# The second unit over tiles of 512 tokens, which may span two batches, in place of halves of 288 tokens of one batch

## The chip, the core and the metric

One core of one Trainium2 chip. The metric is the device time of one execution in microseconds; the value shown for a kernel is the median of its runs. The profile is one further execution of the same program, recorded by the hardware.

## What is computed

Causal attention with a cumulative bias (4 batches, 8 heads, 576 tokens, 64 wide), then a gated unit with a token-mixing matrix (the first unit), then a squared-ReLU unit with a sigmoid gate (the second unit). The second unit, which the change is about, cut to what matters:

```python
B, S, D = x.shape                      # 4, 576, 512: 2304 tokens in all
x_prev = concatenate([zeros((B, 1, D)), x[:, :-1, :]], axis=1)   # the token before, 0 at each batch's start
xk = mu_k * x + (1.0 - mu_k) * x_prev
xr = mu_r * x + (1.0 - mu_r) * x_prev
k = maximum(xk @ w_k, 0.0)             # 512 -> 1024
v = k * k @ w_v                        # 1024 -> 512
r = 1.0 / (1.0 + exp(-(xr @ w_r)))     # 512 -> 512
return r * v
```

## The kernel before

Features lie on the 128 partitions, tokens along the free dimension. Products are made in three terms: each float32 operand is split into a part that the matmul format holds and the remainder ("hi" and "lo"; `split_lo` makes the remainder by a subtraction), and for each 128-row block of the contraction the helper `gemm3` issues hi·hi, lo·hi and hi·lo into one PSUM bank.

Attention (`attn_pair`) and the first unit (`moe1`, one call for each batch b) run interleaved. `moe1(b)` ends with four output blocks: for each m, two halves of 288 tokens are accumulated (`o`), VectorE adds the residual into an SBUF tile `y` of 577 columns, whose column 0 was set to zero by GpSimd, and one DMA writes `y` to the DRAM tensor `ydram[m, :, b]` (L464). The zero column stands for the token before the first.

The second unit starts when attention has given its SBUF back. `late(i)` loads a 512 KB piece of the weights `w_k`, `w_r` or `w_v` (tile `lraw`, two buffers) and converts it from 64-bit words to hi and lo, on ScalarE and VectorE (`convert`, with the tiles `ly` and `lz`). Then, batch by batch:

- `prep(b)`: for each feature block k one DMA brings `yt` (577 columns) from `ydram`; for xk and for xr ScalarE multiplies the shifted columns 0 to 575 (`lt`, L563), VectorE adds the columns 1 to 576 times mu (L564), ScalarE copies the hi part (L565), and the lo part is a subtraction, on VectorE for batch 0 and on GpSimd for the others (L566).
- `k`: for 8 blocks m and 2 halves of 288 tokens, 12 matmuls into a bank, ReLU by ScalarE to `lk`, square by VectorE, hi copy `kh` by ScalarE, lo part `kl` by VectorE.
- `gate(m)` (`r`, sigmoid to `sg`) and `vo`: for 4 blocks m and 2 halves, 12 and 24 matmuls; VectorE multiplies and a DMA writes 576 columns to the output.

That is 192 + 96 + 192 = 480 matmuls of 288 columns for a batch, 1920 in all. The eight PSUM banks are handed out in turn (`bank`); `y`, `lk` and `o` share three SBUF buffers (tag `tmp`), `lt` has four and `yt` two.

All DMAs are issued by SyncE (SP), one queue in program order: an entry whose wait isn't over holds up those behind it. The order on each engine is made by a list scheduler when the program is built, from dependences and its own estimate of time.

Of the kernel before, what the change touches and what calls it, by code (L numbers as in the profile page):

```python
# [37 lines left out]
def fused_kernel(ctx, tc, kqT, vL, s, w_in, g_ln, w_sgT, b_sg, w_out, mu_k, mu_r, w_k, w_v, w_r, out):  # L38
# [5 lines left out]
    ydram = dram.tile([KD, P, B, S + 1], F32, tag="ydram", name="ydram")  # L44
# [314 lines left out]
    def moe1(b):  # L359
# [87 lines left out]
        for m in range(KD):  # L447
# [16 lines left out]
            nc.sync.dma_start(out=ydram[m, :, b], in_=y)  # L464
# [83 lines left out]
    def late(i):  # L548
        src, (hi, lo) = loads[i]
        raw = lw.tile([P, 512, 2], U32, tag="lraw", name=f"lraw{i}", bufs=2)  # L550
        nc.sync.dma_start(out=raw.rearrange("p n c -> p (n c)"), in_=src.bitcast(U32))
        y = lw.tile([P, S], F32, tag="ltmp", name=f"ly{i}", bufs=4)
        t = lw.tile([P, S], F32, tag="ltmp", name=f"lz{i}", bufs=4)
        convert(hi, lo, raw, y[:, :512], t[:, :512].bitcast(U32), nc.vector, low=mhalf[:, 0:1])

    def prep(b):
        xx = [[ep.tile([P, KD, S], F32R, tag=t, name=f"x{t}_{b}") for t in r] for r in (("vn0", "vn1"), ("xs0", "xs1"))]
        for k in range(KD):
            yt = lw.tile([P, S + 1], F32, tag="yt", name=f"yt{b}_{k}", bufs=2)
# [8 lines left out]

    for b in range(B):
        if b == 0:  # L570
            for i in range(8):
# [8 lines left out]
        for m in range(KF):  # L580
            f = slice(m * P, (m + 1) * P)
            if b == 0:
# [1 line left out]
            t = ep.tile([P, S + 1], F32, tag="tmp", name=f"lk{b}_{m}", bufs=3)[:, :S]
# [13 lines left out]
        def gate(m):
            f = slice(m * P, (m + 1) * P)
            sg[m] = ew.tile([P, S], F32, tag="wc", name=f"sg{b}_{m}", bufs=3)  # L600
            for hf in range(2):
                acc = bank(f"r{b}_{m}_{hf}")
                c = slice(hf * HF, (hf + 1) * HF)
                mms = []
                for k in range(KD):
                    mms += [(wr[0][:, k, f], xr[0][:, k, c]), (wr[0][:, k, f], xr[1][:, k, c]), (wr[1][:, k, f], xr[0][:, k, c])]
                gemm3(acc[:, :HF], mms)
                nc.scalar.activation(sg[m][:, c], acc[:, :HF], AF.Sigmoid, scale=1.0 / WS)

        gate(0)  # L610
        for m in range(KD):
# [3 lines left out]
            o = ep.tile([P, S + 1], F32, tag="tmp", name=f"o{b}_{m}", bufs=3)[:, :S]  # L615
            for hf in range(2):
                acc = bank(f"vo{b}_{m}_{hf}")
                c = slice(hf * HF, (hf + 1) * HF)
                mms = []
                for k in range(KF):  # L620
                    mms += [(wvv[0][k][:, f], kk[0][k][:, c]), (wvv[0][k][:, f], kk[1][k][:, c]), (wvv[1][k][:, f], kk[0][k][:, c])]
                gemm3(acc[:, :HF], mms)
                nc.vector.scalar_tensor_tensor(out=o[:, c], in0=acc[:, :HF], scalar=1.0 / WS, in1=sg[m][:, c], op0=ALU.mult, op1=ALU.mult)  # L623
# [48 lines left out]
```

## Time and profile before

| | before |
|---|---|
| median of 3 runs | 714.98 us (714.29 to 715.26) |
| span of the profiled execution | 714.3 us |
| TensorE matmul busy | 674.2 us, 94% |
| VectorE / ScalarE / GpSimd busy | 429.2 / 394.7 / 248.9 us |

In the profile PE is TensorE's matmuls, PEld its weight loads, DVE VectorE, ACT ScalarE, POOL GpSimd, SP SyncE. Times within the execution count from the span's start. Matmuls overlap, so the cost of one within a run of them is the distance between starts, not its listed duration. The granted clock is in shares of 2.4 GHz (1.00 is 2.4 GHz, 0.50 is 1.2 GHz).

### The profile page before, as it was taken

How to read it: one execution, taken by the hardware profiler on the slowest of the kernel's cores; microseconds unless marked ns; L12 is line 12 of the kernel's file. 1: busy time of each engine (PE TensorE's matmuls, PEld its weight loads, DVE VectorE, ACT ScalarE, POOL GpSimd, SP SyncE). 2: the span in 40 equal slices, each digit the busy share in tenths (PEclk: the TensorE clock that was granted, in tenths of full speed). 3: DMA queues.
4: the chain of work that ended last, by engine and by line, in shares of the span. 5: the costliest groups of instructions: out<-in, count | busy, mean ns of one | idle time of the engine just before them, and what ended most of it. 6: DMA issues, size and time to landing. Idle time of an engine off the chain costs nothing.

```text
span 714.3 us, 12830 instructions
## 1 busy us (share of the span) xinstructions
PE 674.2 (94%) x4720; PEld 603.2 (84%) x4720; DVE 429.2 (60%) x952; ACT 394.7 (55%) x911; POOL 248.9 (35%) x243
## 2 busy tenths in 40 slices
PE   2869999999998999999999999999999999999998
PEld 1546767878976888977988999899999999999997
DVE  6876589994668455479733589898434144413411
ACT  4777787874557555367734587598435134512400
POOL 7455555367246268245463130002402030330000
PEclk9989999999999899999999999999999999999999
DMA  7663551552733332742401873652300120000001
GB/s 209 190 220 91 163 151 49 171 159 65 211 94 96 112 83 69 196 127 64 128 15 44 287 237 114 202 171 83 90 30 16 52 68 1 17 33 19 2 21 46
DMA packets 33038, 74.96 MB, mean 105 GB/s; under 512 B 4368, under 2 KB 8464, under 8 KB 32976
## 3 DMA queue, kind: packets, MB, share of 16 engines
q1 hardware_dynamic: 32976, 74.15, 34.4%
q8 instruction: 37, 0.61, 0.4%
q14 instruction: 25, 0.20, 0.1%
HBM read 50.84 MB, written 13.79 MB: 90 GB/s over the span
## 4 chain that ended last, share of the span: by engine, by line
PE 78%; DVE 10%; DMA 5%; issue 2%; POOL 2%; ACT 2%; SPq 0%; DVEq 0%; POOLq 0%; ACTq 0%
PE k L355 14%; PE vo L355 14%; PE pv L326 8%; PE r L355 7%; PE sg L355 6%; PE v L355 5%; PE tp L296 5%; PE o L355 4%; PE u L355 4%; PE sc L247 4%; PE sc L248 3%; DMA kq<-in_kqT_dram 3%; DMA lraw<-in_w_k_dram 2%; DVE st L272 1%; DVE QB L224 1%
## 5 line engine op out<-in xcount | busy, mean ns | idle before, releaser
L355 PE MATMUL k<-xvn,wk 128*128 128x288 f32 x768 | 102.9, 295 | 0.4 <-DVE y L461 0.4
L355 PEld LDWEIGHTS k<-xvn,wk 128*128 128x128 f32 x768 | 102.2, 188 | 0.7 <-DVE y L461 0.7
L247 PE MATMUL sc<-ka,qa 128*128 128x512 f32 (+3 forms) x180 | 64.3, 368 | 26.5 <-DVE mx L272 12.6
L280 ACT ACTIVATE st<-st,mx 128x128 f32<-128x128 f32 (+4 forms) x124 | 72.0, 583 | 21.8 <-DVE mx L272 20.7
L272 DVE CUSTOM_DVE_ANT_0 st<-sc,mask 128x512 f32<-128x512 f32 (+3 forms) x124 | 61.0, 501 | 15.8 <-PE sc L248 12.3
L326 PE MATMUL pv<-pt,vf 128*64 128x320 f32 (+4 forms) x448 | 68.3, 380 | 0.7 <-DVE u L484 0.6
L247 PEld LDWEIGHTS sc<-ka,qa 128*128 128x128 f32 x180 | 33.5, 187 | 41.4 <-DVE mx L272 17.6
L355 PE MATMUL sg<-wsg,vn 128*128 128x288 f32 x448 | 65.2, 298 | 1.2 <-DVE u L484 1.2
L355 PEld LDWEIGHTS sg<-wsg,vn 128*128 128x128 f32 x448 | 60.6, 188 | 2.3 <-DVE u L484 1.5
L623 DVE SCALAR_TENSOR_TENSOR o<-vo,sg 128x288 f32<-128x288 f32 x32 | 14.5, 456 | 79.8 <-PE vo L355 79.6
L66 POOL TENSOR_TENSOR KB<-kq,ka 64x576 fp32r<-64x576 f32 x29 | 44.0, 1516 | 48.9 <-ACT ka L225 44.4
L326 PEld LDWEIGHTS pv<-pt,vf 128*64 128x64 f32 x448 | 36.7, 142 | 27.1 <-issue 7.7
L66 POOL TENSOR_TENSOR xvn<-lt,xvn 128x576 fp32r<-128x576 f32 x12 | 19.8, 1658 | 111.6 <-ACT xvn L565 111.6
L248 PE MATMUL sc<-KB,QB 128*128 128x512 f32 (+3 forms) x180 | 58.5, 337 | 0.0
L355 PE MATMUL vo<-kh,wva 128*128 128x288 f32 x256 | 56.2, 295 | 0.0
L355 PE MATMUL vo<-kh,wvb 128*128 128x288 f32 x256 | 56.1, 295 | 0.0
L66 POOL TENSOR_TENSOR qa<-kq,QB 64x576 fp32r<-64x576 f32 x29 | 43.1, 1486 | 33.7 <-DVE QB L224 21.7
L592 ACT ACTIVATE lk<-k 128x288 f32<-128x288 f32 x64 | 26.2, 409 | 49.0 <-PE k L355 46.9
L355 PE MATMUL r<-xxs,wr 128*128 128x288 f32 x384 | 52.9, 295 | 0.0
L355 PEld LDWEIGHTS r<-xxs,wr 128*128 128x128 f32 x384 | 51.6, 188 | 0.0
L296 PE MATMUL tp<-ident,st 128*128 128x128 f32 x300 | 47.4, 277 | 1.8 <-ACT rb L339 1.4
L355 PE MATMUL v<-wv,xs 128*128 128x512 f32 x192 | 48.7, 397 | 0.0
(176 smaller groups left out, 1566.6 us busy)
## 6 DMA issues: line engine op xcount, KB each, us to landing
wc<-wscr SPq DMA_DIRECT2D x24, 512.0 KB
kq<-in_kqT_dram SPq DMA_DIRECT2D x32, 288.0 KB
vf<-in_vL_dram SPq DMA_DIRECT2D x16, 320.0 KB
ydram<-y SPq DMA_DIRECT2D x16, 288.5 KB
yt<-ydram SPq DMA_DIRECT2D x16, 288.5 KB
out_dram<-o SPq DMA_DIRECT2D x16, 288.0 KB
qa<-QB SPq DMA_DIRECT2D x30, 144.0 KB
ka<-ka SPq DMA_DIRECT2D x30, 144.0 KB
```

The costliest lines, as they stand in the source:

```text
L66: eng.tensor_tensor(out=lo, in0=x, in1=f32(hi), op=ALU.subtract)
L224: (nc.scalar.copy if hd < 2 else nc.vector.tensor_copy)(qb[64:128], kq[64:128])
L247: nc.tensor.matmul(sc[:m, :c1 - c0], qa[:, q], ka[:, c0:c1], start=True, stop=False)
L248: nc.tensor.matmul(sc[:m, :c1 - c0], qb[:, q], kb[:, c0:c1], start=False, stop=True)
L272: nc.vector.tensor_tensor_reduce(out=st[:, c0:c1], in0=sc[:, :n], in1=mk, op0=ALU.add, op1=ALU.min, scale=-SCALE, scalar=mx[:, 0:1] if ci ...
L280: e = nc.scalar.activation(st[:, :w], st[:, :w], AF.Exp, bias=mx[:, last:last + 1], scale=-1.0, accum_out=sm[:, 4 * hh + i % 4:4 * hh + i ...
L296: nc.tensor.transpose(tp[:, c:c + P], st[:, j * P:(j + 1) * P], ident)
L326: nc.tensor.matmul(acc[64 * a:64 * a + 64, o:n], vf[:, a, kk], pt, start=(kk == 0), stop=(kk == nk - 1))
L355: nc.tensor.matmul(acc, a, w_, start=(i == 0), stop=(i == n - 1))
L592: nc.scalar.activation(t[:, c], acc[:, :HF], AF.Relu, scale=1.0 / WS)
L623: nc.vector.scalar_tensor_tensor(out=o[:, c], in0=acc[:, :HF], scalar=1.0 / WS, in1=sg[m][:, c], op0=ALU.mult, op1=ALU.mult)
```

## The change

The second unit no longer goes by batches. The 2304 tokens are taken as one row and cut into four tiles of 512 and one of 256 (`CH`, `TOK`); a tile may hold the end of one batch and the start of the next. Every accumulation covers a whole tile: 96 + 48 + 96 = 240 matmuls a tile, 960 of 512 columns and 240 of 256, and one evacuation in place of two. So that the shifted tokens of a tile that spans two batches can be read without a special case, `ydram` holds y twice: copy 0 the tokens, copy 1 the tokens shifted by one, with the zero at each batch's start. Each `y` tile is therefore written by two DMAs of 288 KB, and `yt` is read as two rows of 512 columns (512 KB; 256 KB for the last tile). The lo parts of `prep` are all made by VectorE.

```diff
-    ydram = dram.tile([KD, P, B, S + 1], F32, tag="ydram", name="ydram")
+    ydram = dram.tile([2, KD, P, B * S], F32, tag="ydram", name="ydram")
...
-            nc.sync.dma_start(out=ydram[m, :, b], in_=y)
+            for i in range(2):
+                nc.sync.dma_start(out=ydram[i, m, :, b * S:(b + 1) * S], in_=y[:, 1 - i:1 - i + S])
...
-            yt = lw.tile([P, S + 1], F32, tag="yt", name=f"yt{b}_{k}", bufs=2)
-            nc.sync.dma_start(out=yt, in_=ydram[k, :, b])
+            yt = lw.tile([P, 2, CH], F32, tag="yt", name=f"yt{c}_{k}", bufs=2)
+            nc.sync.dma_start(out=yt[:, :, :n], in_=ydram[:, k, :, t0:t0 + n].rearrange("i p n -> p i n"))
...
-                nc.scalar.mul(t, yt[:, 0:S], mu[:, r, 1, k:k + 1])
-                nc.vector.scalar_tensor_tensor(out=t, in0=yt[:, 1:S + 1], scalar=mu[:, r, 0, k:k + 1], in1=t, op0=ALU.mult, op1=ALU.add)
-                nc.scalar.copy(xx[r][0][:, k], t)
-                split_lo(nc.gpsimd if b else nc.vector, xx[r][1][:, k], t, xx[r][0][:, k])
+                nc.scalar.mul(t, yt[:, 1, :n], mu[:, r, 1, k:k + 1])
+                nc.vector.scalar_tensor_tensor(out=t, in0=yt[:, 0, :n], scalar=mu[:, r, 0, k:k + 1], in1=t, op0=ALU.mult, op1=ALU.add)
+                nc.scalar.copy(xx[r][0][:, k, :n], t)
+                split_lo(nc.vector, xx[r][1][:, k, :n], t, xx[r][0][:, k, :n])
...
-    for b in range(B):
+    for c in range((TOK + CH - 1) // CH):
+        n = min(CH, TOK - c * CH)
+        t0 = c * CH
...
-            for hf in range(2):
-                acc = bank(f"k{b}_{m}_{hf}")
-                c = slice(hf * HF, (hf + 1) * HF)
-                mms = []
-                for k in range(KD):
-                    mms += [(wk[0][:, k, f], xk[0][:, k, c]), (wk[0][:, k, f], xk[1][:, k, c]), (wk[1][:, k, f], xk[0][:, k, c])]
-                gemm3(acc[:, :HF], mms)
-                nc.scalar.activation(t[:, c], acc[:, :HF], AF.Relu, scale=1.0 / WS)
+            acc = bank(f"k{c}_{m}")
+            mms = []
+            for k in range(KD):
+                xh, xl = (x[:, k, :n] for x in xk)
+                mms += [(wk[0][:, k, f], xh), (wk[0][:, k, f], xl), (wk[1][:, k, f], xh)]
+            gemm3(acc[:, :n], mms)
+            nc.scalar.activation(t, acc[:, :n], AF.Relu, scale=1.0 / WS)
...
-            nc.sync.dma_start(out=out[m, :, b], in_=o)
+            nc.sync.dma_start(out=out[m].rearrange("p b s -> p (b s)")[:, t0:t0 + n], in_=o)
```

`gate` and `vo` change in the same way as `k`.

SP's queue at the place where the first weight pieces are loaded (`y_0` to `y_3` are batch 2's outputs, `wc_` the weights of batch 3's first unit, `lraw` pieces of `w_k`, `yt_` the tokens of the first tile). Before:

```order
L464 DMA ydram<-y_0_4651 128x577
L551 DMA lraw_5335<-in_w_k_dram 128x1024
L551 DMA lraw_5345<-in_w_k_dram 128x1024
L560 DMA yt_0_5419<-ydram 128x577
L560 DMA yt_1_5431<-ydram 128x577
L492 DMA wc_0_4796<-wscr 128x1024
L464 DMA ydram<-y_1_4702 128x577
L551 DMA lraw_5355<-in_w_k_dram 128x1024
```

After:

```order
L465 DMA ydram<-y_0_4659 128x576 x2
L552 DMA lraw_5351<-in_w_k_dram 128x1024
L552 DMA lraw_5361<-in_w_k_dram 128x1024
L566 DMA yt_0_5435<-ydram 128x2x512
L566 DMA yt_1_5447<-ydram 128x2x512
L493 DMA wc_0_4808<-wscr 128x1024
L465 DMA ydram<-y_1_4711 128x576 x2
L552 DMA lraw_5371<-in_w_k_dram 128x1024
```

The sequence is the same; each `y` entry stands twice and each `yt` carries 512 KB where it carried 288.

TensorE's row in the first batch or tile, where `vo` first needs the converted `w_v` (`wva` its first four blocks, `wvb` its last four). Before, at the end of `vo_0`:

```order
L355 MATMUL vo_0_1_5941<-kl_6_5518,wvb_5333 128x288
L355 MATMUL vo_0_1_5941<-kh_6_5513,wvb_5334 128x288
L355 MATMUL vo_0_0_5915<-kh_7_5514,wvb_5334 128x288
L355 MATMUL vo_0_1_5941<-kh_7_5514,wvb_5333 128x288
L355 MATMUL vo_0_1_5941<-kl_7_5519,wvb_5333 128x288
L355 MATMUL vo_0_1_5941<-kh_7_5514,wvb_5334 128x288
L355 MATMUL r_2_0_5969<-xxs_0_5417,wr_5329 128x288
```

After, where `vo_0` first reads `wvb`:

```order
L355 MATMUL r_2_5819<-xxs_0_5434,wr_5345 128x512
L355 MATMUL r_2_5819<-xxs_0_5433,wr_5346 128x512
L355 MATMUL vo_1_5834<-kh_0_5523,wva_5347 128x512
L355 MATMUL vo_0_5791<-kh_4_5527,wvb_5349 128x512
L355 MATMUL vo_0_5791<-kl_4_5532,wvb_5349 128x512
L355 MATMUL vo_1_5834<-kl_5531,wva_5347 128x512
L355 MATMUL vo_1_5834<-kh_0_5523,wva_5348 128x512
L355 MATMUL vo_0_5791<-kh_4_5527,wvb_5350 128x512
```

Before, `r_2` came after the whole of `vo_0`; now its 12 matmuls and half of `vo_1` stand ahead of `vo_0`'s use of `wvb`.

## Rows read from the trace of the kernel before

**Rows 1.** The page: span, busy time (share) xinstructions of two engines.

```profile
span 714.3 us, 12830 instructions
PE 674.2 (94%) x4720; PEld 603.2 (84%) x4720; DVE 429.2 (60%) x952; ACT 394.7 (55%) x911; POOL 248.9 (35%) x243
```

**Rows 2.** Chain that ended last, one batch and the end: start us, us, what.

```profile
583.46 25.49 PE k L355 x192
...
647.12 25.49 PE k L355 x192
...
698.08 12.73 PE vo L355 x96
```

**Rows 3.** PE's waits from 395 to 715 us: us in total, times, longest.

```profile
PE o L355 <- DVE gl L66: 1.8, 1, 1.8
PE k L355 <- DVE y L461: 0.4, 1, 0.4
```

**Rows 4.** Timeline of PE and PEld: start us, us, op, shape, xcount [idle before <-releaser].

```profile
404.49 6.09 PE L355 MATMUL v<-wv,xs 128*128 128x512 f32 x26
410.41 2.02 PE L355 MATMUL v<-wv,xq 128*128 128x512 f32 x8
412.27 12.89 PE L355 MATMUL u<-xs,wc 128*128 128x288 f32 x96
425.00 15.26 PE L355 MATMUL sg<-wsg,vn 128*128 128x288 f32 x112
...
427.78 1.36 PEld L355 LDWEIGHTS sg<-wsg,vn 128*128 128x128 f32 x10 [0.21 <-DVE vn L66]
```

**Rows 5.** Timeline of PE at 219 us, two matmuls of 256 columns.

```profile
219.00 0.28 PE L247 MATMUL sc<-ka,qa 128*128 128x256 f32 x1
219.12 0.28 PE L248 MATMUL sc<-KB,QB 128*128 128x256 f32 x1
```

**Rows 6.** Windows: PE, PEld, DVE, ACT, POOL busy (x), PEclk, DMA share, GB/s.

```profile
402.00:404.00 2.00, 2.00 (x14) 1.83 (x14) 1.77 (x5) 0.88 (x2) 0.00 (x0) 1.00 1.03 403
404.00:406.00 2.00, 2.00 (x12) 1.74 (x12) 1.84 (x5) 1.89 (x2) 0.00 (x0) 1.00 1.02 415
...
446.00:448.00 2.00, 0.45 (x3) 0.45 (x4) 2.00 (x4) 1.53 (x3) 0.10 (x1) 1.00 0.00 0
452.00:454.00 2.00, 1.56 (x12) 1.42 (x11) 2.00 (x7) 1.29 (x3) 0.00 (x0) 1.00 0.98 317
...
570.00:580.00 10.00, 10.00 (x78) 10.00 (x77) 5.54 (x6) 5.71 (x9) 6.71 (x4) 1.00 0.17 52
```

**Rows 7.** Timeline of ACT; in brackets idle us before it and its releaser.

```profile
406.95 0.67 ACT L73 ACTIVATE ly<-lraw 128x512 f32<-128x512 f32 x1 [0.33 <-DMA lraw<-in_w_k_dram]
...
461.40 0.67 ACT L73 ACTIVATE ly<-lraw 128x512 f32<-128x512 f32 x1 [1.81 <-DMA lraw<-in_w_r_dram]
```

**Rows 8.** Timeline of DVE, load stage and first batch.

```profile
433.98 0.75 DVE L66 TENSOR_TENSOR xxs<-lt,xxs 128x576 fp32r<-128x576 f32 x1
...
462.75 0.69 DVE L79 SCALAR_TENSOR_TENSOR lz<-lraw,lz 128x512 uint32<-128x512 uint32 x1 [1.92 <-ACT lz L78]
...
492.53 0.69 DVE L66 TENSOR_TENSOR wvb<-ly,wvb 128x512 fp32r<-128x512 f32 x1
```

**Rows 9.** The end: last piece of the chain that ended last.

```profile
710.89 0.46 DVE o L623
```

**Rows 10.** Timeline of SP from 705 us: start us, us from first to last.

```profile
705.03 6.68 SPq L624 DMA_DIRECT2D out_dram<-o  x2
```

**Rows 11.** Windows of 1 us around a fall of the granted clock, columns as above.

```profile
228.00:229.00 1.00, 0.00 (x0) 0.00 (x0) 1.00 (x5) 0.27 (x1) 1.00 (x1) 1.00 0.44 78
229.00:230.00 1.00, 0.74 (x2) 0.30 (x2) 1.00 (x4) 0.73 (x3) 0.46 (x1) 0.84 0.72 247
231.00:232.00 1.00, 1.00 (x3) 0.22 (x1) 1.00 (x5) 0.09 (x1) 0.22 (x1) 0.50 0.00 0
236.00:237.00 1.00, 1.00 (x7) 0.80 (x6) 0.00 (x0) 0.00 (x0) 0.00 (x0) 0.75 0.00 0
```

More of the change, by code (lines that the diff above doesn't have):

```diff
@@ L551, in late @@
         nc.sync.dma_start(out=raw.rearrange("p n c -> p (n c)"), in_=src.bitcast(U32))
-        y = lw.tile([P, S], F32, tag="ltmp", name=f"ly{i}", bufs=4)
-        t = lw.tile([P, S], F32, tag="ltmp", name=f"lz{i}", bufs=4)
+        y = lw.tile([P, 512], F32, tag="ltmp", name=f"ly{i}", bufs=4)
+        t = lw.tile([P, 512], F32, tag="ltmp", name=f"lz{i}", bufs=4)
         convert(hi, lo, raw, y[:, :512], t[:, :512].bitcast(U32), nc.vector, low=mhalf[:, 0:1])
-    def prep(b):
-        xx = [[ep.tile([P, KD, S], F32R, tag=t, name=f"x{t}_{b}") for t in r] for r in (("vn0", "vn1"), ("xs0", "xs1"))]
+    CH = 512
@@ L558, in prep @@
+    TOK = B * S
+    def prep(c):
+        n = min(CH, TOK - c * CH)
+        t0 = c * CH
+        xx = [[ep.tile([P, KD, S], F32R, tag=t, name=f"x{t}_{c}") for t in r] for r in (("vn0", "vn1"), ("xs0", "xs1"))]
         for k in range(KD):
-            yt = lw.tile([P, S + 1], F32, tag="yt", name=f"yt{b}_{k}", bufs=2)
-            nc.sync.dma_start(out=yt, in_=ydram[k, :, b])
+            yt = lw.tile([P, 2, CH], F32, tag="yt", name=f"yt{c}_{k}", bufs=2)
+            nc.sync.dma_start(out=yt[:, :, :n], in_=ydram[:, k, :, t0:t0 + n].rearrange("i p n -> p i n"))
@@ L572, in fused_kernel @@
                 late(i)
-        xk, xr = prep(b)
-        if b == 0:
+        xk, xr = prep(c)
+        if c == 0:
             for i in range(8, 12):
                 late(i)
-        kh = [ep.tile([P, S], F32R, tag="xT", name=f"kh{b}_{m}", bufs=8) for m in range(KF)]
-        kv = ep.tile([P, KD, S], F32R, tag="v", name=f"kl{b}")
-        kk = [kh, [kv[:, m] for m in range(KD)] + [ep.tile([P, S], F32R, tag="u", name=f"kl{b}_{m}", bufs=4) for m in range(KD, KF)]]
+        kh = [ep.tile([P, S], F32R, tag="xT", name=f"kh{c}_{m}", bufs=8) for m in range(KF)]
@@ L580, in fused_kernel @@
+        kv = ep.tile([P, KD, S], F32R, tag="v", name=f"kl{c}")
+        kk = [kh, [kv[:, m] for m in range(KD)] + [ep.tile([P, S], F32R, tag="u", name=f"kl{c}_{m}", bufs=4) for m in range(KD, KF)]]
         for m in range(KF):
             f = slice(m * P, (m + 1) * P)
[L582 removed]
+            if c == 0:
                 late(12 + m)
[L584 to L592 removed]
+            t = ep.tile([P, S + 1], F32, tag="tmp", name=f"lk{c}_{m}", bufs=3)[:, :n]
+            acc = bank(f"k{c}_{m}")
[5 more added lines that the diff above has]
+            nc.scalar.activation(t, acc[:, :n], AF.Relu, scale=1.0 / WS)
@@ L593, in fused_kernel @@
             nc.vector.tensor_tensor(out=t, in0=t, in1=t, op=ALU.mult)
-            nc.scalar.copy(kk[0][m], t)
-            split_lo(nc.vector, kk[1][m], t, kk[0][m])
+            nc.scalar.copy(kk[0][m][:, :n], t)
+            split_lo(nc.vector, kk[1][m][:, :n], t, kk[0][m][:, :n])
         sg = {}
@@ L599, in gate @@
             f = slice(m * P, (m + 1) * P)
[L600 to L608, printed above, removed]
+            sg[m] = ew.tile([P, S], F32, tag="wc", name=f"sg{c}_{m}", bufs=3)[:, :n]
+            acc = bank(f"r{c}_{m}")
+            mms = []
+            for k in range(KD):
+                xh, xl = (x[:, k, :n] for x in xr)
+                mms += [(wr[0][:, k, f], xh), (wr[0][:, k, f], xl), (wr[1][:, k, f], xh)]
+            gemm3(acc[:, :n], mms)
+            nc.scalar.activation(sg[m], acc[:, :n], AF.Sigmoid, scale=1.0 / WS)
         gate(0)
@@ L614, in fused_kernel @@
             f = slice(m * P, (m + 1) * P)
[L615 to L623, printed above, removed]
-            nc.sync.dma_start(out=out[m, :, b], in_=o)
+            o = ep.tile([P, S + 1], F32, tag="tmp", name=f"o{c}_{m}", bufs=3)[:, :n]
+            acc = bank(f"vo{c}_{m}")
+            mms = []
+            for k in range(KF):
+                kx = [t[k][:, :n] for t in kk]
+                mms += [(wvv[0][k][:, f], kx[0]), (wvv[0][k][:, f], kx[1]), (wvv[1][k][:, f], kx[0])]
+            gemm3(acc[:, :n], mms)
+            nc.vector.scalar_tensor_tensor(out=o, in0=acc[:, :n], scalar=1.0 / WS, in1=sg[m], op0=ALU.mult, op1=ALU.mult)
+            nc.sync.dma_start(out=out[m].rearrange("p b s -> p (b s)")[:, t0:t0 + n], in_=o)
 def kernel(**inputs):
```

6 lines of the change are left out of this document (4 added, 2 removed).

## The prediction, made before the changed kernel ran

> **What bounds the kernel now.** I read the page first: PE is busy for 94% of the span, DVE for 60% [rows 1]. Then the chain that ended last. Its whole second half is PE: the k part of a batch takes 25.49 us for 192 matmuls, one batch follows the other without a gap, and the last piece before the end is PE's again [rows 2]. From 583.46 to 647.12 us one batch of 480 matmuls takes 63.66 us, that is 132.6 ns each. Third, PE's waits from 395 us on: 1.8 us and 0.4 us, both while batch 3's first unit ends, and none after that [rows 3]. So the second unit is bound by PE alone, and its time is the number of matmuls times the distance between two of them. What the change makes of that distance is the main question; the second is whether the stage ahead, in which weights are loaded and converted, keeps up.
>
> **The distance at 512 columns.** The kernel already has matmuls of 512 columns with the same types and weight shape: in the run of v, 26 of them take from 404.49 to 410.41 us, 227.7 ns each; right after, the 96 of u take from 412.27 to 425.00 us, 132.6 ns each at 288 columns, and PEclk is 1.00 in both [rows 4, 6]. 224 more columns cost 95.1 ns, 0.4245 ns a column, which leaves 132.6 - 288 x 0.4245 = 10.3 ns that a matmul costs whatever its width. For 256 columns this line gives 119.0 ns. Two matmuls of 256 columns stand 0.12 us apart [rows 5], which agrees.
>
> Before: 4 x 63.66 = 254.6 us. After: 960 x 0.2277 + 240 x 0.119 = 218.6 + 28.6 = 247.2 us. **Term 1: -7.5 us**, all on the path. It is the 720 matmuls fewer at 10.3 ns each; the number of columns is the same. Bounds: the 256-column matmul is not seen in a long run, so it lies between 117.9 (u's distance by columns) and 132.6 ns (no cheaper than 288), 28.3 to 31.8 us. For the 512 columns the next row, 8 matmuls from 410.41 to 412.27 us [rows 4], gives 232.5 ns and with it 4.6 us more; I take the 26, because the 8 end with the change to another stage and the 26 are the longest run.
>
> The Trainium skill, page "TensorE: Matmul & The Clock Gate", section "Back-to-back issue gap", gives N/2.4 + 2.5 ns for a warm matmul. By that the change removes only 720 x 2.5 = 1.8 us. The rows here lie 10 to 12 ns above it at both widths (132.6 against 122.5, 227.7 against 215.8), so this trace does not agree, and I go by the rows.
>
> **What feeds PE in the second unit.** These edits I cost at nothing. An accumulation takes 12 x 0.228 = 2.7 us and is now evacuated once instead of twice; an operation over 128x512 takes 0.6 to 0.7 us [rows 7, 8]. The lo parts of three batches' prep leave POOL for DVE. In the stretch where they ran, 570 to 580 us, DVE was busy 5.54 and POOL 6.71 of 10 us [rows 6]; four subtractions of about 0.7 us [rows 8] in place of POOL's four make DVE busy for some 8.4 of 10. That still fits, and prep has the 33 us of gate and vo (144 x 0.228) before PE needs its result. If this cover were gone, PE would wait at a tile's start for about 1 us, four times. The yt reads grow from 288 to 512 KB at a DMA share of 0.17 [rows 6].
>
> **Ahead of the second unit.** Prep of the first tile goes over 512 columns instead of 576. A subtraction takes 0.75 us over 576 and 0.68 to 0.69 over 512 columns [rows 8], so some 0.07 us each. Twelve such DVE operations of prep stand ahead of the place where PE waits 1.8 us for gl on DVE, which is busy without a gap there (2.00 of 2 us) [rows 3, 6]. **Term 2: -0.8 us**; it can't bring more than the 2.2 us of waits and could bring nothing.
>
> At the end DVE evacuates 256 columns instead of 288 (0.46 us now [rows 9]), and the last DMA, issued at about 711.4 us [rows 10], carries 128 KB instead of 288; 160 KB at about 400 GB/s [rows 6] are 0.4 us. **Term 3: -0.4 us.**
>
> **What the second copy of y costs.** 16 more DMAs of 288 KB, on SP's queue. Nobody waits for them but the three SBUF buffers that y shares with lk and o, and whatever stands behind them in the queue. Up to 395 us PE's row is full, and I cost the copies there at nothing. They matter at two places.
>
> First, the load stage. DMA is full from 402 to 406 us (share 1.03 and 1.02, 403 and 415 GB/s) [rows 6]. Ahead of the third piece of w_k there are now 0.30 MB more of y_1 and twice 0.23 MB more of yt, 0.75 MB, 1.8 us at 410 GB/s; with y_2 and y_3, 1.34 MB, 3.3 us. ACT already waits 0.33 us for that piece [rows 7], so the delay reaches DVE, which does the statistics and vn of the first unit in the same queue. sg, started at 425.00 us, waits 0.21 us at 427.78 us for the last part of vn [rows 4]: no slack. Between nothing (DVE's gaps before 427 us swallow it) and 3.3 us I take **term 4: +1.0 us**, about half of the 1.8 us, since the later pieces are issued only when a buffer is converted.
>
> Second, the first tile. Three more copies (0.88 MB) stand ahead of the last w_r piece and of w_v; at 317 GB/s [rows 6] that is 2.8 us. DVE already waits 1.92 us there, because ACT waits 1.81 us for that piece [rows 7, 8]. From then on DVE works through to the last wvb at 493.2 us [rows 8]. After the change PE is sooner where it needs w_v, but the order has changed too: with r_2 and half of vo_1 ahead of it, PE first reads the last wvb 176 matmuls after k's start. With the start at about 452.6 us (in the windows PE idles 0.44 of 452 to 454 us just before it [rows 3, 6]) and 24 matmuls of o at 132.6 ns between, that is 452.6 + 3.2 + 176 x 0.2277 = 495.9 us. DVE's 16 operations on lk and kl are shorter by 0.07 us each: 493.2 - 1.1 + 2.8 = 494.9 us. It fits by one microsecond, so nothing; without that microsecond PE waits one-for-one, up to 2.8 us.
>
> **Sum**, against the profiled execution: 714.3 - 7.5 - 0.8 - 0.4 + 1.0 = 706.6 us. The median of the runs lies 0.6 us above this span, so the forecast is 707.2 us.
>
> **Rivals.**
>
> 1. The 10.3 ns belong to the columns, not to the matmul (a slower stream in the second unit, as the 232.5 ns of the eight suggest). Then 512 columns cost 132.6 x 512/288 = 235.7 ns, term 1 is zero, and the time is 714.3 - 0.8 - 0.4 + 1.0 + 0.6 = 714.7 us. For it: eight matmuls. Against it: 26 in a run, and 288 against 512 columns in neighbouring rows at the same clock. 5 in 100. The page's rule, as a mechanism of this kernel (of the 12.6 ns above 120 ns most follow the columns), would be its neighbour, at 712.9 us; I count it in here.
>
> 2. Part of the gain is eaten by a stall. The order on PE differs from about 300 us on, and the load stage may be late by the full 3.3 us. What a stall can cost the trace shows once: around 228 us PE idles for more than 1 us, from 229.7 us PEclk falls to 0.50, and it is back in the course of 236 to 237 us [rows 11]: 6.8 us at half speed, 3.4 us of work lost. One late load stage, 2.3 us beyond term 4, gives 709.5 us; with the fall of the clock 712.9 us. For it: the full DMA rows and sg without slack. Against it: the idle 1.55 of 2 us at 446 to 448 us left PEclk at 1.00 [rows 6]. 17 in 100.
>
> 3. Slower than before: the extra bytes starve the weight conversion at both places, and each time the clock falls. 3.3 + 3.4 in the load stage and 2.8 + 3.4 in the first tile are 12.9 us, against 8.7 us of gains (terms 1 to 3): 714.3 - 8.7 + 12.9 + 0.6 = 719.1 us. It decides when both delays come through in full and each leaves PE idle for longer than at 446 us. 7 in 100.
>
> 4. Better: the waits of 2.2 us vanish whole and the load stage isn't late: 714.3 - 7.5 - 2.2 - 0.4 + 0.6 = 704.8 us. 8 in 100 at or below it.
>
> That the change doesn't do what it says is no case: the program's rows on PE hold matmuls of 512 and 256 columns.
>
> **How the numbers follow.** 63 in 100 for the forecast with its own range of 705 to 709.5 us. A measurement of this kernel can tell about 0.2%, 1.4 us, from no change: 713.6 to 716.4 us. The range of 704.7 to 712.9 us takes in the forecast, rival 2 and the upper half of rival 4 and leaves out rivals 1 and 3 and what lies below. Faster: forecast, rivals 2 and 4 and a little of 1, 0.86. Same: the rest of rival 1 and mixtures of stalls, 0.07. Slower: 0.07.
>
> **What would show it.** The k part of a tile of 512 taking 96 x 227.7 ns = 21.9 us, a tile 54.6 us, and the last tile 28.6 us, without waits on PE after its first k, show term 1 right; a tile of over 56.5 us shows rival 1. Term 2: PE's wait for gl below 1.8 us. Term 4: sg starting later relative to u, with a wait for vn, and ACT waiting longer for lraw; rival 2 and 3 show as PEclk below 1.00 anywhere after 240 us. The first tile is right if PE shows no wait for wvb. I would be wrong above all if the first tile starts much later than 452 us, or if PE idles anew between 300 and 395 us.

## The result, and the profile of the changed kernel

The changed kernel takes 708.17 us (median of 6 runs, 706.47 to 710.63), the kernel before 714.5 us beside it. The ratio is 0.9908 with an interval of 0.9884 to 0.9933: faster by 0.9%, 6.3 us. Timed twice more beside the kernel before, it took 708.47 and 707.90 us (x1 and x9 below, ratios 0.9911 and 0.9906). The forecast was 707.2 us.

The page of the profiled execution, two lines that answer to [rows 1]:

```profile
span 704.5 us, 11476 instructions
PE 668.2 (95%) x4000; PEld 556.6 (79%) x4000; DVE 438.4 (62%) x996; ACT 396.0 (56%) x899; POOL 210.8 (30%) x219
```

PE's share is what it was: the second unit is still bound by PE alone. The chain that ended last shows the third tile of 512 and the last tile, of 256 (start us, us, what; left-out lines are further r and vo of the same kind):

```profile
561.88 22.40 PE k L355 x96
584.28 5.60 PE r L355 x24
589.88 5.47 PE vo L355 x24
...
606.41 10.91 PE vo L355 x48
...
672.76 11.31 PE k L355 x96
684.07 2.83 PE r L355 x24
686.89 2.88 PE vo L355 x24
...
695.48 5.77 PE vo L355 x48
```

In the kernel before, the rows of r and vo that go with the k of [rows 2] are:

```profile
608.95 6.38 PE r L355 x48
615.33 6.36 PE vo L355 x48
...
634.41 12.71 PE vo L355 x96
```

Dividing each row by its count: at 512 columns k and r take 233.3 ns, vo 227 to 228 ns. At 256 columns it is the other way round: k and r 118 ns, vo 120 ns. At 288 columns, before, all three took 132.4 to 132.9 ns. So the three parts have not gained alike:

| second unit | before | after | gain | by the prediction's 227.7 and 119.0 ns |
|---|---|---|---|---|
| k | 4 x 25.49 = 101.96 us | 4 x 22.40 + 11.31 = 100.91 us | 1.05 us | 3.1 us |
| r | 4 x 12.74 = 50.96 us | 4 x 11.20 + 5.67 = 50.47 us | 0.49 us | 1.5 us |
| vo | 4 x 25.43 = 101.72 us | 4 x 21.85 + 11.53 = 98.93 us | 2.79 us | 2.9 us |

PE's waits from 395 us to the end (us in total, times, longest), to be read against [rows 3]:

```profile
PE o L355 <- DVE gl L66: 1.0, 2, 0.6
PE k L355 <- DVE y L461: 0.3, 1, 0.3
```

There is no new wait, neither of sg for vn nor of vo for `wvb`, and nothing after the first k. To see where the rest went, the execution is cut at the first matmul of a stage (v, o: first unit of the batch in brackets; k: second unit). Times in us, from one profiled execution each; x1 and x9 are the changed kernel again, the other columns are experiments told below.

| stretch | before | after | x1 | x9 | x2 | x3 | x11 | x10 |
|---|---|---|---|---|---|---|---|---|
| start to v(1) | 194.97 | 193.56 | 195.26 | 196.87 | 194.47 | 195.56 | 193.46 | 194.39 |
| v(1) to o(1) | 82.48 | 81.07 | 79.52 | 81.12 | 81.15 | 81.12 | 79.52 | 77.58 |
| o(1) to v(2) | 24.43 | 24.03 | 24.05 | 24.02 | 24.03 | 24.55 | 24.03 | 24.02 |
| v(2) to o(3) | 138.21 | 137.31 | 137.28 | 137.29 | 137.34 | 140.02 | 137.35 | 137.13 |
| o(3) to first k | 12.49 | 11.56 | 12.61 | 12.58 | 14.58 | 11.13 | 11.94 | 13.52 |
| first k to last vo | 257.91 | 253.43 | 253.42 | 253.42 | 258.62 | 253.40 | 253.41 | 253.42 |

The last line is the same to 0.03 us in all columns with the wide tiles: the second unit gains 4.5 us (the table of k, r and vo adds up to 4.3). Stretches 3 and 4 repeat to 0.03 us in the three executions of the changed kernel: 1.3 us less than before. The first, second and fifth differ between executions of one program by up to 3.3, 1.6 and 1.1 us, so a single pair of profiles says little there. The lines add up: from before to after the spans differ by 9.8 us, of which 2.8 us lie ahead of o(1), where the three executions of one program scatter as much; the medians differ by 6.3 us. Half of the 2.8 us is there from the start: PE's first matmul begins at 12.12 us before and at 10.63 us after. The other half is the granted clock: it is at 0.50 from 229.7 us for 6.8 us in the one profile of the kernel before [rows 11], but for 3.4 us in the first of the changed kernel, and also in x3, which has the PE rows of the kernel before and 81.12 us in that stretch.

### The profile page after: what moved, and what is told of

Same layout as the page of the kernel before. It is cut to its first block, busy times and chain, and to the rows that moved or that the text cites. A ratio compares the mean times of both kernels' runs of the same rounds, so it can differ in the third digit from the quotient of the medians.

```text
span 704.5 us, 11476 instructions
## 1 busy us (share of the span) xinstructions
PE 668.2 (95%) x4000; PEld 556.6 (79%) x4000; DVE 438.4 (62%) x996; ACT 396.0 (56%) x899; POOL 210.8 (30%) x219
## 4 chain that ended last, share of the span: by engine, by line
PE 80%; DVE 11%; DMA 3%; ACT 2%; issue 2%; POOL 1%; SPq 0%; DVEq 0%; ACTq 0%; POOLq 0%
PE k L355 14%; PE vo L355 14%; PE pv L326 8%; PE r L355 7%; PE sg L355 7%; PE v L355 6%; PE o L355 6%; PE tp L296 4%; PE sc L247 4%; PE u L355 4%; PE sc L248 3%; DVE st L272 1%; DVE QB L224 1%; DMA lraw<-in_w_k_dram 1%; DMA sraw<-in_w_in_dram 1%
## 5 line engine op out<-in xcount | busy, mean ns | idle before, releaser
L355 PE MATMUL k<-xvn,wk 128*128 128x512 f32 (+1 forms) x480 | 102.0, 373 | 0.3 <-DVE y L461 0.3
L355 PEld LDWEIGHTS k<-xvn,wk 128*128 128x128 f32 x480 | 83.6, 188 | 17.7 <-DVE y L461 0.5
L326 PE MATMUL pv<-pt,vf 128*64 128x320 f32 (+4 forms) x448 | 66.7, 375 | 1.3 <-DVE u L485 1.2
L355 PE MATMUL r<-xxs,wr 128*128 128x512 f32 (+1 forms) x240 | 53.4, 373 | 0.0
L599 ACT ACTIVATE lk<-k 128x512 f32<-128x512 f32 (+1 forms) x40 | 22.2, 557 | 51.9 <-PE k L355 48.5
L355 PE MATMUL vo<-kh,wva 128*128 128x512 f32 (+1 forms) x160 | 49.0, 369 | 0.0
L355 PE MATMUL vo<-kh,wvb 128*128 128x512 f32 (+1 forms) x160 | 48.8, 368 | 0.0
L355 PEld LDWEIGHTS r<-xxs,wr 128*128 128x128 f32 x240 | 42.0, 188 | 8.5
L628 DVE SCALAR_TENSOR_TENSOR o<-vo,sg 128x512 f32<-128x512 f32 (+1 forms) x20 | 12.6, 636 | 57.9 <-PE vo L355 57.9
L296 PEld LDWEIGHTS tp<-ident,st 128*128 128x128 f32 x300 | 35.9, 143 | 8.0 <-ACT st L280 2.8
```

The lines of the kernel that those rows point to most:

```text
L296: nc.tensor.transpose(tp[:, c:c + P], st[:, j * P:(j + 1) * P], ident)
L326: nc.tensor.matmul(acc[64 * a:64 * a + 64, o:n], vf[:, a, kk], pt, start=(kk == 0), stop=(kk == nk - 1))
L355: nc.tensor.matmul(acc, a, w_, start=(i == 0), stop=(i == n - 1))
L599: nc.scalar.activation(t, acc[:, :n], AF.Relu, scale=1.0 / WS)
L628: nc.vector.scalar_tensor_tensor(out=o, in0=acc[:, :n], scalar=1.0 / WS, in1=sg[m], op0=ALU.mult, op1=ALU.mult)
```

## The experiments

**x1 and x9: the changed kernel again.** No edit.

> The changed kernel once more, to part what the change does from what differs between executions. In the first pair of profiles the changed kernel was already 1.4 us ahead at the first matmul of batch 0's o, where both programs still issue the same rows, and 3.9 us ahead at batch 3's v. Theory A (the lead before the second unit is a matter of the execution: how often and how long the granted clock falls in attention): here the first k starts anywhere from 447 to 452 us and moves with the clock, while from the first k to the last vo stays within 0.3 us of 253.8 us. Rival B (the new order in attention gains it): the first k again starts at 447 to 448 us with the same clock as before.

> The changed kernel once more, as the neighbour of the next runs on one chip. 708.2 us, within 706.5 and 709.5.

Measured: 708.47 us (705.65 to 709.11; ratio 0.9911, 0.9887 to 0.9935) and 707.90 us (704.25 to 710.99; ratio 0.9906, 0.9883 to 0.9930). In both profiles PE's waits before the first k are larger than in the first one; of x1:

```profile
PE o L355 <- DVE gl L66: 2.0, 2, 1.4
PE k L355 <- DVE y L461: 0.3, 1, 0.3
```

This is what the kernel before shows too (1.8 and 0.4 us, [rows 3]). The shorter wait of the first profile is one execution's luck, not yet a gain of the change. The first k starts at 448.7 and 451.9 us, against 447.5 us in the first profile, and from the first k on nothing moves: most of the early lead was the execution, as theory A has it. Its reason, the falls of the clock, is not all of it: in x9 PE's first matmul begins 2.1 us later than in the first profile, and the two falls behind it are as long in both (10.2 and 3.4 us). What repeats of rival B is the 1.3 us of stretches 3 and 4.

**x2: the kernel before, every y written twice.** The second write goes to a tensor that nobody reads.

```diff
             nc.sync.dma_start(out=ydram[m, :, b], in_=y)
+            nc.sync.dma_start(out=ycopy[m, :, b], in_=y)
```

> The kernel before with every y written to DRAM twice, the second time to a place that nobody reads; matmuls, reads and tiles as before. Theory A (the second write is hidden; term 4 was sized too high): ratio to before 1.000 within 0.002, the first k within 1 us of its place in the kernel before, sg of batch 3 without a new wait. Rival B (the bytes delay the weight pieces, term 4 as forecast, and are paid back elsewhere): 1 to 3 us slower, ratio 1.0015 to 1.004, with a longer wait of ScalarE for lraw and of PE for vn or gl.

Measured: 716.01 us (714.41 to 717.44, 12 runs), ratio 1.0018 (1.0004 to 1.0031). PE's waits from 395 us on:

```profile
PE o L356 <- DVE gl L67: 2.7, 2, 2.4
PE o L356 <- ACT gh L445: 0.9, 1, 0.9
PE o L356 <- DMA wc<-wscr: 0.5, 1, 0.5
```

The table above tells two things in one column. The bytes do delay the stage before the second unit: o(3) to k takes 14.58 us instead of 12.49, and the stretch from the first k on is 0.7 us longer, of which 0.5 us is PE's wait for `wc`, after the first matmuls of k. But stretches 3 and 4 have the changed kernel's times, 1.3 us less than before, although nothing else was edited. In the built programs PE's first 1695 rows of x2 and of the changed kernel are alike (equal neighbours count as one row; in the trace this is up to 407 us), while those of the kernel before differ from both at the 671st (at about 189 us). The second write is the only edit, so it is what made the list scheduler give out another order.

**x3: the changed kernel with one copy of y.** The copy is one row of 2305 columns, from which both the tokens and the shifted tokens are read; GpSimd sets the product to zero at the starts of batches.

```diff
-            for i in range(2):
-                nc.sync.dma_start(out=ydram[i, m, :, b * S:(b + 1) * S], in_=y[:, 1 - i:1 - i + S])
+            nc.sync.dma_start(out=ydram[m, :, b * S + p0:(b + 1) * S + 1], in_=y[:, p0:])
...
+                for s0 in range(S, TOK, S):
+                    if t0 <= s0 < t0 + n:
+                        nc.gpsimd.memset(t[:, s0 - t0:s0 - t0 + 1], 0.0)
```

> The changed kernel with y in DRAM once, as 2305 columns: a tile of 512 reads 513 columns, and where a batch starts inside the tile GpSimd sets that column of the product with mu to zero. Same outputs. Tiles and matmuls as in the changed kernel. Theory A (the copies cost nothing): within 0.2% of the changed kernel, that is a ratio to before of 0.989 to 0.993. Rival B (the copies cost the 1 us of term 4 or more): 1 to 3 us faster than the changed kernel, ratio 0.985 to 0.989. If it is slower by more than 0.2%, the three waits on GpSimd a batch start are on the path.

Measured: 710.03 us (709.21 to 712.15), ratio 0.9941 (0.9920 to 0.9962): 1.6 us above the changed kernel on the same chip (x1; each of the six runs is above each of x1's), with half the writes. The second unit is as fast (253.40 us) and o(3) to k is the shortest in the table (11.13 us). The loss stands in stretches 3 and 4, and in a wait that the changed kernel does not have:

```profile
PE sg L355 <- DVE vn L66: 1.8, 1, 1.8
```

Its first 1794 rows on PE (up to 441 us) are those of the kernel before. The kernel before, with the same rows, doesn't show this wait, so the 1.8 us are not PE's order alone.

**x11: x3 with every y written a second time, to a tensor that nobody reads.**

```diff
             nc.sync.dma_start(out=ydram[m, :, b * S + p0:(b + 1) * S + 1], in_=y[:, p0:])
+            nc.sync.dma_start(out=ycopy[m, :, b * S:(b + 1) * S], in_=y[:, 0:S])
```

> The kernel with a single copy of y of 2305 columns (x3), in which every y is written a second time to a tensor that nobody reads; the tiles are made from the single copy, and nothing is left out. The scheduler's order of TensorE's rows is that of the changed kernel up to the 1695th row (310 us) and that of the kernel before in x3. If the loss of x3 is the order: this one has x2's and the changed kernel's faster stages from batch 2 on (24.0 us from o of batch 1 to v of batch 2 instead of 24.5, 137.3 us from there to o of batch 3 instead of 140.0) and 708 us, so a second write that nobody needs makes the kernel faster by 1.5 to 2 us. If it is the zeroing on GpSimd or the form of the reads: 710 us as x3, or more.

Measured: 707.92 us (704.97 to 709.41), ratio 0.9910 (0.9896 to 0.9924). Writes that serve nothing take 2.1 us off x3 (two chips; the ratios to the kernel before fall from 0.9941 to 0.9910). Stretches 3 and 4 are the changed kernel's, 24.03 and 137.35 us, and o(3) to k grows by 0.8 us. So x3's loss, the wait of sg included, was the order that the scheduler gave out, not the zeroing and not the reads. Which engine's order made sg wait is open.

**x6 and x10: the changed kernel with four writes of every y**, two of them unread, on two chips.

```diff
                 nc.sync.dma_start(out=ydram[i, m, :, b * S:(b + 1) * S], in_=y[:, 1 - i:1 - i + S])
+                nc.sync.dma_start(out=ycopy[i, m, :, b * S:(b + 1) * S], in_=y[:, 1 - i:1 - i + S])
```

> The changed kernel with two further writes of every y to a DRAM tensor that nobody reads, so four writes for each y instead of two; nothing is left out. If the writes of y cost nothing because they lie beside other work: 708.2 us as the changed kernel, within 0.2%. If they cost what the doubled writes cost the kernel before (1.3 us for 16 more DMAs): 32 more DMAs give 710 to 711 us, with PE's waits for gl and gh before the second unit's first k above 2 us in total. If the load stage was at its limit (the prediction's term 4 in full): 711.5 us and more, with a wait of sg for vn.

> Four writes of every y instead of two, timed before at 705.5 us on another chip; nothing is left out. What it gained lies before 271 us, in the first two batches, where the scheduler has put TensorE's rows into another order from the 661st on, and where the clock did not fall at 230 us. If the order is the cause, it is faster than the changed kernel here too, by 2 to 3 us, with no fall of the clock at 230 us in the profile. If it was that chip or that execution: the same as the changed kernel within 0.2%.

Measured: 705.54 us (ratio 0.9876, 0.9848 to 0.9905) and 706.08 us (ratio 0.9881, 0.9867 to 0.9896). This is the fastest version of all, and no theory had it so in x6; x10 falls just short of its 2 to 3 us. On x10's chip the changed kernel itself took 707.90 us, 1.8 us more; the intervals of the two ratios still touch. PE's waits of x10 from 395 us on show that the bytes cost something here too:

```profile
PE o L356 <- DVE gl L67: 2.1, 1, 2.1
PE k L356 <- DVE y L462: 1.0, 1, 1.0
```

The gain is in v(1) to o(1): 77.58 us, and 77.60 in x6. Its PE rows part from those of all other kernels at the 662nd (at 186 us). The windows around 228 us tell what that does (us, busy of PE, PEld, DVE, ACT, POOL, then PEclk, DMA share, GB/s). The changed kernel, first profile:

```profile
226.00:228.00 2.00, 0.65 (x4) 0.38 (x3) 2.00 (x5) 0.69 (x2) 1.92 (x2) 1.00 0.63 133
228.00:230.00 2.00, 1.62 (x5) 0.94 (x4) 2.00 (x8) 1.03 (x4) 0.82 (x3) 0.68 0.23 89
230.00:232.00 2.00, 2.00 (x8) 0.65 (x9) 1.08 (x5) 1.32 (x3) 0.81 (x1) 0.50 0.00 0
```

The changed kernel again, x1:

```profile
228.00:230.00 2.00, 0.65 (x3) 0.30 (x2) 2.00 (x6) 0.98 (x3) 1.68 (x2) 1.00 0.60 144
230.00:232.00 2.00, 1.61 (x9) 0.88 (x10) 2.00 (x7) 0.73 (x3) 0.78 (x2) 1.00 0.12 46
```

Four writes, x10:

```profile
220.00:222.00 2.00, 1.19 (x9) 0.93 (x8) 2.00 (x9) 1.93 (x5) 1.40 (x1) 1.00 0.74 207
222.00:224.00 2.00, 1.30 (x6) 0.63 (x5) 2.00 (x8) 2.00 (x9) 1.62 (x3) 1.00 0.50 203
224.00:226.00 2.00, 1.81 (x10) 1.11 (x11) 2.00 (x6) 2.00 (x6) 1.33 (x1) 1.00 0.16 37
226.00:228.00 2.00, 1.60 (x12) 1.04 (x12) 1.94 (x7) 1.89 (x6) 1.15 (x2) 1.00 0.20 42
```

In the changed kernel PE idles for 1.35 of 2 us, and the clock falls to half in one execution and stays in another. In x10's order PE's idle time is more spread out, 0.81 of 2 us at most in these windows, and neither x6 nor x10 shows a fall. Against x1, which had no fall either, the order is worth 1.9 us in this stretch. That it also keeps the clock up is suggested by two profiles and not shown: of the ten profiles with the changed kernel's PE rows up to here (x2, x4, x5, x7, x8, x11 and x12 among them) two, x1 and x11, have no fall either.

**x4: w_k and w_v change places in SBUF.** Of a matmul's two operands the 128x128 one that PEld loads is called stationary, the other is streamed. In the built programs w_k lies at bytes 155,200 to 187,968 of each partition, w_r from there to 204,352, and w_v at 19,456 to 58,880; x4 puts w_k where w_v was and w_v where w_k was.

```diff
-    wk = [lw.tile([P, KD, DFF], F32R, tag=f"wk{i}", name=f"wk{i}") for i in range(2)]
+    wvl = [lw.tile([P, KF, DM], F32R, tag=f"wk{i}", name=f"wvl{i}") for i in range(2)]
...
+    wk = [[wva[i], wvb[i]] for i in range(2)]
```

> In the changed kernel k and r run at 233.5 ns a matmul of 512 columns and vo at 227.0, though form and types are the same; v runs at 227 and its last 8, whose weights lie in another buffer, at 233.5. Here w_k and w_v change places in SBUF (w_k where w_v was, in the buffers of the first unit, w_v in the pool of the second unit); w_r stays. Theory A (the place of the weights sets the distance): k falls to 227 ns, r stays at 233.5, vo rises to 233.5. Rival B (the moving side, or what the other engines do in the k part): k stays at 233.5 and vo at 227. The time as a whole is worse, since w_k can only be loaded when the first unit no longer needs its buffers; I expect the first k 10 to 25 us later.

Measured: 710.28 us, one run. The chain of waits, one tile of 512:

```profile
565.66 21.79 PE k L355 x96
587.44 5.60 PE r L355 x24
593.04 5.60 PE vo L355 x24
...
609.84 11.20 PE vo L355 x48
```

k is now at 227.0 ns and vo at 233.3 ns; r, not touched, stays at 233.3 ns. What k and vo stream has not moved. So the place of the stationary weights sets the distance at 512 columns. What it is about the place is open. The places with 233 ns are high in SBUF, but each of them also starts 64 bytes past a multiple of 128, and each of those with 227 ns starts on one; no run parts the two.

The first k did not come 10 to 25 us later: it starts at 447.32 us, but after 8 matmuls PE goes on with the first unit, idles for 2.42 us until its weights have landed, and the clock falls:

```profile
447.32 2.00 PE L355 MATMUL k<-xvn,wva 128*128 128x512 f32 x8
451.74 0.40 PE L355 MATMUL o<-gh,wc 128*128 128x288 f32 x1 [2.42 <-DMA wc<-wscr]
```

```profile
452.00:454.00 2.00, 2.00 (x13) 2.00 (x13) 0.09 (x1) 0.15 (x1) 0.10 (x1) 0.72 1.03 360
454.00:456.00 2.00, 2.00 (x10) 2.00 (x9) 1.05 (x2) 0.02 (x1) 0.00 (x0) 0.50 1.03 400
```

From the first k to the last vo it takes 257.30 us, 3.9 us more than the changed kernel: the idle time and 3.4 us at 0.50. This is the stall that the prediction's rivals 2 and 3 spoke of; the changed kernel has none here.

**x8: w_r in low places** (58,880 to 80,384), in exchange sg and the second half of kl above 212,000.

```diff
-    wr = [lw.tile([P, KD, DM], F32R, tag=f"wr{i}", name=f"wr{i}") for i in range(2)]
+    wrh = [ew.tile([P, 2, DM], F32R, tag="wc", name=f"wrh{i}", bufs=3) for i in range(2)]
+    wr = [[wrh[k // 2][:, k % 2] for k in range(KD)], [ep.tile([P, DM], F32R, tag="u", name=f"wrl{k}", bufs=4) for k in range(KD)]]
...
-... ep.tile([P, S], F32R, tag="u", name=f"kl{c}_{m}", bufs=4)
+... lw.tile([P, CH], F32R, tag="kl", name=f"kl{c}_{m}", bufs=4)
...
-            sg[m] = ew.tile([P, S], F32, tag="wc", name=f"sg{c}_{m}", bufs=3)[:, :n]
+            sg[m] = lw.tile([P, CH], F32, tag="sg2", name=f"sg{c}_{m}", bufs=3)[:, :n]
```

> The changed kernel with w_r's hi and lo parts put into low places of SBUF (58,880 to 80,384 bytes per partition, where the first unit's weights and gl lie) and with sg and the second half of kl put into the weights' region above 212,000 in exchange; nothing is left out. If the place of the stationary weights sets the distance at 512 columns: r takes 226 to 228 ns instead of 233.5, 192 x 6.3 ns = 1.2 us less over the four wide tiles, k stays at 233.5. If the rows r and k are slow for another reason (what streams, the number of rows in the bank, the stage): r stays at 233.5. The total depends also on when w_r can be converted, since its new places come free later: 707 us without a new wait, 709 to 711 us with one at the first r.

Measured: 709.84 us (706.85 to 710.57), ratio 0.9920 (0.9892 to 0.9949), not told apart from the changed kernel. The chain, one tile:

```profile
506.72 22.40 PE k L355 x96
529.12 5.45 PE r L355 x24
534.58 5.49 PE vo L355 x24
540.07 2.76 PE r L355 x12
...
551.08 11.03 PE vo L355 x48
```

r falls to 227.1 ns in the row of 24 and to 230 ns in those of 12; k stays at 233.3 ns. That much was expected. But vo rises from 227.3 to 229.8 ns in the row of 48, and its weights did not move: it streams half of kl from a high place now (from 212,544, again 64 bytes past a multiple of 128, where it lay on one). So the place of what is streamed counts too. Per tile r gains 0.23 us and vo loses 0.16 us, so the 1.2 us were not to be had in this way. PE has no wait at the first r, so by its own terms the time should have been 707 us; the runs scatter over 3.7 us and leave that open.

**x5: tiles of 256 tokens.**

```diff
-    CH = 512
+    CH = 256
```

> The changed kernel with tiles of 256 tokens, nine of them, in place of four of 512 and one of 256; nothing is left out. The last tile of the changed kernel, the one of 256, took 28.5 us. Theory (the distance has a fixed part and a part by columns, and which it is depends on where the stationary weights lie): 117.8 ns for k and r and 120.2 ns for vo, 28.5 us a tile, 9 x 28.5 = 256.5 us and 3.2 us of the first unit's o in the first tile, 259.7 us from the first k on against the 253.4 us of the changed kernel, so 6.3 us slower than it (714.5 us): the gain of the change is gone. Rival (the line of the prediction, 10.3 ns a matmul everywhere): 9 x 240 x 119.0 ns = 257.0 us against 247.2 us, 10 us slower than the changed kernel, 718 us. A second tile's start that PE has to wait for (prep of a tile has half the time) would show as waits on PE at the tiles' starts.

Measured: 716.73 us (715.30 to 718.78), ratio 1.0027 (1.0008 to 1.0046). One tile in the chain, and the one new wait of the first tile:

```profile
598.49 11.31 PE k L355 x96
609.80 2.83 PE r L355 x24
612.62 2.88 PE vo L355 x24
...
621.21 5.76 PE vo L355 x48
```

```profile
PE vo L355 <- ACT wvb L84: 4.0, 4, 1.3
```

Each tile takes 28.5 us, k and r 118 and vo 120 ns a matmul, as the theory of places has it. The 4.0 us of waiting for `wvb` were in no expectation: a first tile of half the length reaches w_v before it is converted. They more than cover the 2.2 us by which the time lies above the 714.5 us; what made up for the rest was not looked for. With tiles of 512 it fits, as the prediction worked out.

**x7: the lo parts of xr of the first tile on GpSimd.**

```diff
-                split_lo(nc.vector, ...)
+                split_lo(nc.gpsimd if c == 0 and r else nc.vector, ...)
```

> The changed kernel with one edit: the lo parts of xr of the first tile (four subtractions over 512 columns) are made on GpSimd instead of VectorE; nothing is left out. If VectorE's queue is what TensorE's 1.0 us of waiting for gl before the second unit rests on (term 2 of the prediction), the wait goes, and the kernel is up to 1 us faster than the changed kernel (707.2 us). If it is something else that ends last there (the transfers, ScalarE), no difference within 0.2%. If GpSimd is too slow for r of the first tile, TensorE waits anew at r and the kernel is slower by about 1 us.

Measured: 709.55 us (706.85 to 712.56), ratio 0.9924 (0.9897 to 0.9951): not faster. PE's waits ahead of the first k are 1.3 us for gl, 0.9 us anew for gh on ACT and 0.3 us for y, and o(3) to k takes 13.24 us. PE's rows changed as well (from the 1895th), so the unloading of DVE is not seen by itself.

**x12: the lo parts of tiles 1 to 4 on GpSimd, as before the change.**

```diff
-                split_lo(nc.vector, ...)
+                split_lo(nc.gpsimd if c else nc.vector, ...)
```

> The changed kernel with the lo parts of xk and xr of tiles 1 to 4 on GpSimd again, as in the kernel before; nothing is left out. TensorE's rows are the same in both. If that move costs and brings nothing, as the prediction has it: the same time within 0.2%, k following vo without a gap at every tile. If VectorE was at its limit in the second unit, this one is faster by up to 4 us; if GpSimd's port or its slower subtraction delays a tile, slower, with TensorE waiting at the first k of tiles 1 to 4.

Measured: 707.69 us (706.37 to 708.85), ratio 0.9901 (0.9886 to 0.9917): the same as the changed kernel. Windows over one tile, columns as above, first the changed kernel, then x12:

```profile
507.00:562.00 55.00, 55.00 (x240) 44.80 (x239) 24.92 (x39) 21.28 (x36) 0.00 (x0) 1.00 0.24 70
```

```profile
507.00:562.00 55.00, 55.00 (x240) 44.73 (x239) 23.48 (x32) 23.36 (x38) 12.93 (x9) 1.00 0.24 74
```

PE is full in both, with DVE at 45% of the tile. The move between the engines costs and brings nothing.

## Why the prediction was right, and where it was not

**What bounds the second unit** was right: PE alone, one tile behind the other without a gap, no wait for `wvb` in the first tile, and the evacuations and prep hidden.

**Term 1, -7.5 us, measured -4.5 us.** The step that failed is the one that took 227.7 ns, the distance of the 26 matmuls, for all 960. For vo it is right (2.8 us gained, 2.9 expected). k and r, three fifths of the matmuls, take 233.3 ns, and 576 matmuls by 5.6 ns are the 3.2 us that are missing. The row beside it, 8 matmuls at 232.5 ns [rows 4], was set aside as the end of a stage. In the changed kernel the same 8 stand between rows of u (timeline of PE) and take (408.68 - 406.81) / 8 = 234 ns again:

```profile
406.81 2.03 PE L355 MATMUL v<-wv,xq 128*128 128x512 f32 x8
408.68 5.59 PE L355 MATMUL u<-xs,wc 128*128 128x288 f32 x41
```

And in batch 1 of the kernel before, where the same 8 end a stage as well, they take (216.44 - 214.63) / 8 = 226 ns:

```profile
214.63 1.98 PE L355 MATMUL v<-wv,xq 128*128 128x512 f32 x8
216.44 0.19 PE L247 MATMUL sc<-ka,qa 128*128 128x64 f32 x1
```

So the end of the stage is not the reason. The stationary operand of these 8 is `xq`, which takes whichever of the three buffers of the tag `tmp` is next: in the built programs it starts at byte 147,968 in batch 1 and at 150,304 in batch 3. For k the cause is shown by x4 (w_k and w_v changed places, 233.3 to 227.0 ns), for r by x8. Put as lines through 256 and 512 columns, vo costs 13 ns and 0.42 ns a column, k and r with their weights in high places 2.5 ns and 0.45 ns a column: there the fixed part that the wide tiles were to save hardly exists. So rival 1 ("the 10.3 ns belong to the columns") came near the truth for k and r, 233.3 ns against its 235.7, and was false of vo; it was given 5 in 100 as all or nothing, and its evidence was set aside. The two figures for 512 columns in the Trainium skill, page "TensorE: Matmul & The Clock Gate", section "Back-to-back issue gap" (216 ns for a matmul by itself, 131 ns sustained), agree with no row here, before or after.

**Term 2, -0.8 us, and term 4, +1.0 us**, meet in the same stretch, o(3) to the first k:

| o(3) to first k, us | one write of y | two writes | four writes |
|---|---|---|---|
| prep over 576 columns | 12.49 (before) | 14.58 (x2) | |
| prep over 512 columns | 11.13 (x3) | 11.56, 12.61, 12.58 (after, x1, x9), 11.94 (x11), 10.99 (x12) | 12.82, 13.52 (x6, x10) |

x7 and x8, with two writes and other edits that reach this stretch, take 13.24 and 13.12 us. By these pairs the second write costs 0.8 us (x3 to x11) to 2.1 us (before to x2), and the shorter prep brings 1.4 us (before to x3) to 2.3 us (x2 to the mean of the changed kernel, 12.25 us). Both signs are the forecast's; the sizes are not shown, since they rest on single executions, five with two writes lie 1.6 us apart, and x3 had waited 1.8 us at sg just before the stretch. Together the two terms make -0.2 us in the changed kernel (12.49 to 12.25), where the prediction had +0.2 us. The place of term 4 was wrong: sg has no wait for vn in the changed kernel; the delay comes at o, through gl.

**Term 3, -0.4 us, measured -0.25 us**: from the last vo's start to the span's end 3.84 us before, 3.59 us after (3.38 to 3.62 us in the other kernels with this last tile). DVE's last operation takes 0.42 us instead of 0.46 [rows 9]; that the rest comes from the smaller last transfer is argued, not measured.

**What was costed at nothing and was not**: the copies ahead of 395 us. PE's row is full there, and the bytes cost nothing to be seen; but two entries in the queue in place of one changed the order that the scheduler gave out from batch 1 on, and this order is 1.3 us shorter between o(1) and o(3). x2 has the same gain without the wide tiles, and x11 against x3 shows it in the time. The prediction had the order on PE differ from about 300 us on (rival 2); it differs from about 189 us on.

**From the sum to the time.** The 0.6 us from span to median mixes two things. In each run the time is about 2 us more than that run's span, so the profiled execution of the kernel before was some 1.2 us slower than the median run. Against the medians the forecast was 7.8 us faster and the measured gain is 6.3 us: -4.5 (second unit), -1.3 (order), -0.2 (o(3) to k) and -0.25 (end) make -6.3 us. That this fits so well is luck, since all four are read against one profile of the kernel before, which lies above its own median. It is luck too that 707.2 us lies only 1.0 us from 708.2 us: the order, which nobody forecast, made up for 1.3 of the 3.0 us missing in term 1.

**Rivals 2 and 3** did not happen. The fall of the clock at 230 us was there before the change [rows 11], and it comes and goes between executions of the changed kernel (after and x9 with it, x1 without).

## What to carry to other kernels

A distance between matmuls is read for each pair of operands, at the width that is planned, and an odd row next to a long one is a second case until its reason is known; the same row elsewhere in the trace (here batch 1's) can refute a reason at once. Where a scheduler makes the order, any added queue entry can move work far from the edit by more than the entry costs; compare the order of the whole program, and run a version with a dummy entry to tell the edit from the order. A stretch that differs between two executions of the same program carries no argument from one pair of profiles.

## What the runs showed of the hardware that was not expected

- The distance of matmuls of 512 columns (fp32r, 128x128 stationary, full clock) depends on where the operands lie. It is 227 ns with w_v or w_k at bytes 19,456 to 58,880 of the partition and 233 ns with either of them from 155,200 up (x4, both ways). Half of kl streamed from 212,544 up made vo 229.8 ns instead of 227.3 (x8). At 256 columns the weights in the high places are the faster ones, 118 against 120 ns, again both ways in x4; at 288 columns the difference is at most 0.5 ns.
- Which property of the place does this was not tried. Height is one reading. Another is the start: every buffer with the longer distance at 512 columns starts 32 or 64 bytes past a multiple of 128, those with 227 ns on a multiple. `xq` hints at the second: with it at 150,304 (32 past) or 152,640 (64 past) the 8 matmuls take 232 to 234 ns where they run in a row, and at 147,968, on a multiple of 128 and only 2.3 KB lower, 226 ns in batch 1 of the kernel before and of the changed kernel. But at the same 147,968 they take 231 ns in batch 0 of these executions (the first of the 8 left out), so this doesn't decide it.
- The granted clock falls around 230 us in some executions of a program and not in others, with the same rows on PE and the same longest idle time just before, 1.35 us in the first profile of the changed kernel, in x1 and in x11, of which only the first has the fall. Such a fall (PEclk 0.68 and 0.50 in two windows of 2 us) makes the stretch from v(1) to o(1) 1.6 us longer: 81.07 and 81.12 us against 79.52 us in x1.
